# One kernel of retention attention, a gated MLP and capped expert routing: VectorE and ScalarE in written order in its first part

## The chip, the cores and the metric

The kernel runs on one core of a Trainium2 chip. The metric is device time in microseconds (us), from the kernel's start to its end. Times of one kernel are the median of several runs; the profile shows one execution of its own.

## The reference

Three stages on float32 data, each on the output of the last:

```
scores = q @ k^T / 8                        # 8 batches x 8 heads, 576 x 64
ret    = scores * gamma[h]^(i-j), i >= j    # decay, causal
x      = (ret @ v)  -> 4608 tokens x 512
a, b   = x @ w1, x @ w2                     # w1, w2: 512 x 1024
x      = ((a * b) @ w3) @ w_out             # w3: 1024 x 1024, w_out: 1024 x 512
logits = x @ w_gate                         # 8 experts
# tokens assigned greedily by descending logit, 576 tokens to an expert
out[tokens of e] = relu(x @ w1[e]) @ w2[e]  # expert widths 512 -> 1024 -> 512
```

w1, w2, w3 and w_out come as 64-bit words that hold double-precision values; the kernel makes pairs of 32-bit numbers of them, a rounded high part and a remainder.

## The kernel before

**Tiling.** The 4608 tokens are 36 attention tiles of 128 tokens; three tiles make a block of 384 (`TB`, 12 blocks). Attention is computed in chunks of 64 tokens with a running state, so tile t+1 needs the state of tile t. The MLP's first half, `ab(i)`, is one block's projections: for each of eight slices f of 128 columns one group of 12 matmuls for w1, copied out by ScalarE (L556), and one for w2, multiplied by that copy on VectorE (L558). Each matmul group goes over four row chunks and three products of high and low parts (L549).

**One attention tile** is a set of helpers: `att_scale` (two VectorE scalings, L261), `att_T` (transposes on TensorE, two copies on ScalarE, L276), `att_P` and `att_QK` (matmuls), `att_mask` (two VectorE products, L288), `att_state` (L310, L312), `att_AV` (L321, L329), `att_out` (ScalarE copy L337, VectorE sums L343 and L350, ScalarE rounding L344 and L349, GpSimd remainder L345). The output goes to the token block's x, in high and low parts. In `attention()` the step of tile t issues AV of t, then P, QK and mask of t+1, then the output of t, then the state of t+1 and the scaling and transposes of t+2.

**One weight unit** is 128 x 512 numbers. `conv(u)` makes it: magnitude on ScalarE (L196), clamp (L197), shift (L198), merge of sign (L200) and of low bits (L202) on VectorE, rounding copy on ScalarE (L215), remainder on VectorE (L216). Units are w1 and w2 in turn, slices 0 to 7 (16 units), then eight of w_out and sixteen of w3. A 1 MB load (`load_pair`) brings two slices of w1 or w2; four such loads have buffers at a time. `LEAD` says how many units ahead of its first use `ab(0)` converts.

**Order.** The Python program issues work from generators that `merge` and `turns` interleave by stated costs. That is the order of the program; the scheduler of the framework then orders each engine's instructions by its own model, with the program's order as priority, so that an engine may get a later instruction ahead of an earlier one. Each engine executes its queue in that order. The loads are issued from SP's queue (`ORDER`, then the calls in the generators). `begin()` is the first part: attention tiles 0 to 2 beside conversions, then block 0's projection beside tiles 3 to 5, then the rest of block 0 beside half of block 1; then `w34_all`, which converts w_out and w3, multiplies them, and is interleaved with blocks 1 to 3.

Of the kernel before, what the change touches and what calls it, by code (L numbers as in the profile page):

```python
# [15 lines left out]
TB, NB = 384, 12  # L16
PT = 96
EARLY, LATE0 = 4, 8
LEAD = (3, 4, 4, 4, 4, 4, 4, 4)
LATE = 1.25  # L20
TRIPS = 8
ROUNDS = ((0, 6), (-4, 6), (-4, 6), (-4, 6), (-5, 6))
ORDER = "q0 c0 k0 v0 c1 q1 k1 w0 v1 w1 q2 k2 v2 w2 w3 c2"
Q0 = 10
RAT = (0.75, 0.45, 0.35, 0.36)

# [58 lines left out]
def build(ctx, tc, io):  # L85
# [75 lines left out]
    raws = {}  # L161
# [19 lines left out]

    w3f = {}

    def conv(u):
        raw = raws.pop(u)
        lo, hi = raw[:, :, :, 0], raw[:, :, :, 1]
        if u[0] == "w3":
            b = 2048 + 512 * nxt("cv3", 2)
            ta = raw_t[:, b:b + 512]
        else:  # L190
            b = 512 * nxt("cv", 6)
            ta = tmp_t[:, b:b + 512]
        out = ta
        ta = ta.rearrange("p (k f) -> p k f", k=4)
        tb = hi.bitcast(F32)
        A.activation(ta, hi.bitcast(F32), AF.Abs)  # L196
        V.tensor_scalar(ta, ta, HIGH, LOW, op0=OP.min, op1=OP.max)  # L197
        V.tensor_scalar(ta.bitcast(I32), ta.bitcast(I32), 3, 0x3FFFFFF8,  # L198
                        op0=OP.logical_shift_left, op1=OP.bitwise_and)
        V.scalar_tensor_tensor(tb.bitcast(I32), hi, -1073741824, ta.bitcast(I32),  # L200
                               op0=OP.bitwise_and, op1=OP.bitwise_or)
        V.scalar_tensor_tensor(ta.bitcast(I32), lo, 29, tb.bitcast(I32),  # L202
                               op0=OP.logical_shift_right, op1=OP.bitwise_or)
        n, i, j = u
        if n == "w3":
            w3f[u] = out
            return
        hs, ls = SLOT(n)
        if n == "wo":
            hd, ld = hs[:, i, :], ls[:, i, :]  # L210
            fl = out
        else:
            hd, ld = (x[:, :, 128 * i:128 * i + 128] for x in (hs, ls))
            fl = ta
        A.activation(hd, fl, AF.Copy)  # L215
        V.tensor_tensor(ld, fl, hd.bitcast(F32), op=OP.subtract)  # L216


    qkv = [[A0[:, 1024 * j + 512 * i:1024 * j + 512 * i + 512] for j in range(3)] for i in range(2)]
# [8 lines left out]

    qkT = [A1[:, 1024 * i:1024 * i + 1024].rearrange("p (j c t) -> p j c t", j=2, c=4) for i in range(2)]
    AM = [A1[:, 2048 + 256 * i:2304 + 256 * i] for i in range(2)]  # L230
    ft = A1[:, 2560:3072].rearrange("p (s n) -> p s n", s=2)
    fk = [ft.rearrange("p s (u a i) -> p u s a i", u=2, a=2)[:, i] for i in range(2)]
    Sb = [A2[:, 768 + 256 * i:1024 + 256 * i] for i in range(3)]
    NT = N // 128

    loaded = set()

    def att_load(t, which=(0, 1, 2), eng=SP):
        for i in which:
            if t >= NT or (t, i) in loaded:  # L240
                continue
            loaded.add((t, i))
            x, src = buf(t)[i], (q, k, v)[i]
            p = 0
            while p < 128:
                b, s = divmod(128 * t + p, S)
                n = min(128 - p, S - s)
                if i == 2:
                    eng.dma_start(x[p:p + n].rearrange("p (h d) -> p h d", h=H),
                                 src[b, :, s:s + n, :].rearrange("h s d -> s h d"))  # L250
                else:
                    for r in range(2):
                        eng.dma_start(x[p:p + n].rearrange("p (c r d) -> p r c d", c=4, r=2)[:, r],
                                     src[b, 4 * r:4 * r + 4, s:s + n, :].rearrange("h s d -> s h d"))
                p += n

# [28 lines left out]

    def att_mask(t):
        for s in range(2):
            V.tensor_tensor(AM[s].rearrange("p (c i) -> p c i", c=4),  # L288
                            PYb[s][:, 0:256].rearrange("p (c i) -> p c i", c=4),
                            C("mask")[:, None, :].to_broadcast([128, 4, 64]), op=OP.mult)  # L290

# [22 lines left out]
    def att_AV(t):  # L314
        us = [u for u in range(2) if (2 * t + u) % 9]
        x = qkT[t % 2]
        for u in us:
            for a in range(2):
                for s, b in QUADS:
                    c = 2 * a + b  # L320
                    PE.matmul(PYb[s][halves(b), 256 + 128 * u + 64 * a:320 + 128 * u + 64 * a],  # L321
                              Sb[(2 * t + u) % 3][halves(s), 64 * c:64 * c + 64], x[halves(s), 0, c, halves(u)],
                              start=True, stop=True, skip_group_check=True)
        for s in range(2):
            for a in range(2):
                for u, b in QUADS:
                    c = 2 * a + b
                    k = 2 * s + a
                    PE.matmul(PX[u][halves(b), 64 * k:64 * k + 64],  # L329
                              buf(t)[2][halves(u), 256 * s + 64 * c:256 * s + 64 * c + 64],  # L330
                              AM[s][halves(u), 64 * c:64 * c + 64], start=True, stop=True, skip_group_check=True)

    def att_out(t):
        j, o = divmod(t, 3)
# [14 lines left out]
                A.activation(xh, po, AF.Copy)  # L349
                V.tensor_tensor(xl, po, xh.bitcast(F32), op=OP.subtract)  # L350

    def attention():
        def T(t):
            if t < NT:
                att_scale(t)
                att_T(t)
                if t != 2:
                    att_load(t + (3 if t < 2 else 2), (0,))
        T(0)
        T(1)  # L360
        att_P(0)
        att_QK(0)
        att_mask(0)
        att_state(0)
        yield 2500
        for t in range(NT):
# [10 lines left out]
            att_load(t + 3, (1,))  # L377
            if t != 2:
                att_load(t + (3 if t < 2 else 2), (2,))
            yield 1400  # L380


# [55 lines left out]
        V.tensor_reduce(WG[:, m, 0:8], p[:, :128].rearrange("p (c e) -> p e c", c=4)[:, :8], axis=AX.X, op=OP.add)  # L438
        yield 300

    units = [(n, i, 0) for i in range(8) for n in ("w1", "w2")] + [("wo", i, 0) for i in range(8)]
    units += [("w3", m, h) for m in range(8) for h in range(2)]
    nload = [0]
    nconv = [0]
# [1 line left out]
    def load_more(upto):  # L446

        upto = min(upto, len(units))
        n = 2 * ((upto - 1) // 4) + 2 if upto <= 16 else upto - 8
        while nload[0] < n:  # L450
            if nload[0] < 8:
                load_pair(nload[0])
            else:
                conv_load(units[nload[0] + 8])
            nload[0] += 1

    def conv_next():
        i = nconv[0]
        if i >= len(units):
            return False  # L460
        conv(units[i])
        nconv[0] += 1
        if i == 3:
# [5 lines left out]
        return True  # L469

    def conv_some(n):
        for _ in range(n):
            conv_next()
            yield 2500

    def w34_all():

        while nconv[0] < 25:
            conv_next()
            yield 2600  # L480
        hl = [w34_T(0, 0)]
        gate = None
        for m in range(8):
            for u in (2 * m + 1, 2 * m + 2):
                if u < 16:
                    conv_next()
                    hl.append(w34_T(*divmod(u, 2)))
                    yield 2600
            p = mm_bank()
# [44 lines left out]
    def ab(i):  # L534
# [3 lines left out]
        for f in range(8):  # L538
            fs = slice(128 * f, 128 * f + 128)
            for is_b in range(2):  # L540
                wh, wl = SLOT(("w1", "w2")[is_b])
                if i == 0:
                    need = units.index((("w1", "w2")[is_b], f, 0)) + LEAD[f]
                    while nconv[0] < min(need, 16):
                        conv_next()
# [5 lines left out]
                if not is_b:  # L551
                    if pend is not None:
                        split_g(i, pend)
                        pend = None
                    a = at_[nxt("a", 2)]
# [11 lines left out]
                yield 1960  # L567
        if pend is not None:
            split_g(i, pend)

# [479 lines left out]
            scat.append(st)  # L1050


    att = attention()
    PER = 3
    W34RATE = 1.0

# [24 lines left out]
        if side:  # L1081
            yield from side

    def turns(n, *gens):

        gens = list(gens)
        while gens:
            for g in gens[:]:
                for _ in range(n):
                    c = next(g, None)  # L1090
                    if c is None:
                        gens.remove(g)
                        break
                    yield c

    def begin():
        merge(take(6), conv_some(LEAD[0]), RAT[0])
        a0, a1 = ab(0), ab(1)
        s = take(2 * PER)
        merge(take_from(a0, 8), s, RAT[1])  # L1100
        drain(s)
        merge(turns(2, a0, take_from(a1, 8)), take(1), RAT[2])
        w = w34_all()
        merge(mix(a1, take(2 * PER - 1), 0.8), w, W34RATE)
        for i in range(2, EARLY):
            merge(mix(ab(i), take(2 * PER), RAT[3]), w, W34RATE)
        drain(w)
# [93 lines left out]
```

## Time and profile before

| what | value |
|---|---|
| median of 3 runs | 1313.09 us (1308.81 to 1315.04) |
| profiled execution | 1313.27 us, of which span 1311.2 us |
| busy in the span | TensorE 1257.6 us (96%), VectorE 530.5 (40%), ScalarE 461.0 (35%), GpSimd 253.8 (19%) |
| mean granted TensorE clock | 0.977 |
| TensorE in the first slice of 40 (32.8 us each) | busy 5 tenths, clock 7 tenths |
| in the second and third | 7 and 8 tenths, clock 7 and 9 tenths |
| VectorE in slices 1 to 4 | 6, 7, 9 and 6 tenths |

Busy time is the time in which an instruction of the engine runs. The span goes from the first to the last instruction; a slice is a fortieth of it. The granted clock is a share of TensorE's full speed, 1.00 at 2.4 GHz and 0.50 at 1.2.

### The profile page before, as it was taken

What the parts mean: (1) busy time and instruction counts of PE and PEld (TensorE: products, weight loads), DVE (VectorE), ACT (ScalarE), POOL (GpSimd) and SP (SyncE); (2) the same over time, 40 slices, a digit from 0 to 9 for tenths busy, and PEclk for the clock granted to TensorE, in tenths of its full rate; (3) what the DMA queues carried; (4) which work ended last, traced back from release to release, by engine and by line L of the source; (5) the groups of instructions that cost most, each with busy time, mean ns of one, the idle gap of its engine ahead of it and who ended that gap; (6) DMA issues with size and microseconds to landing.
All of it is one profiled execution on the core that took longest, in us unless ns stands there. A gap on an engine that the chain in (4) does not pass through costs nothing. (4 is left out here: it accounts for less than half of the span.)

```text
span 1311.2 us, 27175 instructions
## 1 busy us (share of the span) xinstructions
PE 1257.6 (96%) x11406; PEld 1114.9 (85%) x11406; DVE 530.5 (40%) x1298; ACT 461.0 (35%) x989; POOL 253.8 (19%) x238
## 2 busy tenths in 40 slices
PE   5789999999999999999999999879999999999996
PEld 4678988889898989889899777669989989899885
DVE  6796454433231312212212555453534425435220
ACT  4443333333322232212221544243434434435321
POOL 0101211112211120202011743331121211211011
PEclk7798999999999999999999999989999999999999
DMA  8766544422312131424012312163433525435110
GB/s 237 224 162 183 146 130 130 121 59 74 82 34 73 25 82 25 136 94 119 10 48 97 113 45 93 43 193 113 153 99 119 163 71 153 133 101 153 49 37 28
DMA packets 156382, 136.00 MB, mean 104 GB/s; under 512 B 119264, under 2 KB 119520, under 8 KB 155232
## 3 DMA queue, kind: packets, MB, share of 16 engines
q1 hardware_dynamic: 150368, 115.35, 30.1%
q0 software_dynamic: 5888, 18.88, 4.4%
q8 instruction: 91, 1.49, 0.5%
q14 instruction: 35, 0.29, 0.1%
HBM read 107.19 MB, written 27.00 MB: 102 GB/s over the span
## 5 line engine op out<-in xcount | busy, mean ns | idle before, releaser
L549 PE MATMUL p<-x,ws 128*128 128x384 f32 x2304 | 426.4, 341 | 1.1 <-POOL x L345 0.9
L549 PEld LDWEIGHTS p<-x,ws 128*128 128x128 f32 x2304 | 400.1, 189 | 9.4 <-issue 3.3
L1035 PE MATMUL p<-ws,g 128*128 128x512 f32 x864 | 218.1, 394 | 1.9 <-DVE rs L1045 1.4
L1035 PEld LDWEIGHTS p<-ws,g 128*128 128x128 f32 x864 | 156.6, 188 | 31.5 <-DVE rs L1045 1.8
L896 PE MATMUL p<-ws,x 128*128 128x512 f32 x576 | 141.8, 401 | 0.0
L896 PEld LDWEIGHTS p<-ws,x 128*128 128x128 f32 x576 | 105.7, 190 | 20.7 <-issue 0.4
L558 DVE TENSOR_TENSOR g<-p,ms 128x384 f32<-128x384 f32 x88 | 49.0, 557 | 181.7 <-PE p L549 173.6
L933 DVE TENSOR_TENSOR ws<-x,ws 128x512 fp32r<-128x512 f32 x120 | 80.9, 690 | 96.9 <-ACT ws L932 96.7
L261 POOL TENSOR_TENSOR a<-a,cst 128x512 f32<-128x512 f32 x52 | 54.8, 1053 | 302.4 <-DMA a<-q 239.7
L932 ACT ACTIVATE ws<-x 128x512 fp32r<-128x512 f32 x128 | 78.5, 630 | 72.3 <-DMA x<-ew 57.2
L556 ACT ACTIVATE ms<-p 128x384 f32<-128x384 f32 x96 | 46.9, 489 | 152.9 <-PE p L549 151.0
L345 POOL TENSOR_TENSOR x<-a,x 128x256 fp32r<-128x256 f32 x64 | 48.9, 775 | 262.5 <-ACT x L344 262.5
L1046 POOL DMA_INDIRECT out<-rs,idx x40 | 40.4, 1010 | 266.0 <-ACT g L1022 145.9
L601 PE MATMUL p<-ws,g 128*128 128x512 f32 x288 | 71.9, 398 | 0.0
L601 PEld LDWEIGHTS p<-ws,g 128*128 128x128 f32 x288 | 52.5, 188 | 13.3 <-issue 2.5
L1013 PE MATMUL p<-a,ws 128*128 128x320 f32 (+1 forms) x384 | 58.3, 301 | 0.5 <-ACT a L996 0.5
L1022 ACT ACTIVATE g<-py 128x256 fp32r<-128x256 f32 x96 | 31.5, 328 | 76.0 <-PE py L1013 67.4
L1013 PE MATMUL py<-a,ws 128*128 128x320 f32 (+1 forms) x384 | 57.4, 298 | 0.0
L1013 PE MATMUL py<-x,ws 128*128 128x320 f32 (+1 forms) x384 | 56.4, 296 | 0.3 <-DVE g L1023 0.3
L1013 PEld LDWEIGHTS p<-a,ws 128*128 128x128 f32 x384 | 55.0, 193 | 1.9 <-ACT a L996 0.7
L1013 PEld LDWEIGHTS py<-a,ws 128*128 128x128 f32 x384 | 54.9, 191 | 1.9
L1013 PE MATMUL p<-x,ws 128*128 128x320 f32 (+1 forms) x384 | 56.6, 297 | 0.0
(189 smaller groups left out, 1483.9 us busy)
## 6 DMA issues: line engine op xcount, KB each, us to landing
x<-ew SPq DMA_DIRECT2D x128, 256.0 KB, 3.1
y_scratch<-ms SPq DMA_DIRECT2D x36, 256.0 KB, 2.0
a<-k SPq DMA_DIRECT2D x64, 128.0 KB, 3.8
ws<-w SPq DMA_DIRECT2D x8, 1024.0 KB, 9.3
a<-q SPq DMA_DIRECT2D x62, 128.0 KB, 2.8
a<-v SPq DMA_DIRECT2D x31, 256.0 KB, 4.0
g_scratch<-g SPq DMA_DIRECT2D x8, 768.0 KB, 4.0
g<-g_scratch SPq DMA_DIRECT2D x4, 1536.0 KB, 6.8
```

Of the source, the lines that this page charges most:

```text
L261: (V if t < Q0 else G).tensor_tensor(xx, xx, tb_[:, :, None].to_broadcast([128, H, DH]), op=OP.mult)
L345: G.tensor_tensor(xl.rearrange("p (s a) i -> p s a i", s=2), f, xh.bitcast(F32).rearrange("p (s a) i -> p s a i", s=2), op=OP.subtract)
L549: PE.matmul(p[:, :TB], w[:, kk, fs], x[:, kk, :], start=(kk == 0 and j == 0), stop=(kk == 3 and j == 2))
L556: A.activation(a, p[:, :TB], AF.Copy)
L558: V.tensor_tensor(g[:, f, :], p[:, :TB], a, op=OP.mult)
L601: PE.matmul(p, x[:, f, ts], w[:, f, :], start=(f == 0 and j == 0), stop=(f == 7 and j == 2))
L896: PE.matmul(p, x[:, f, :], w[:, f, :], start=(f == 0 and j == 0), stop=(f == 7 and j == 2))
L932: A.activation(h, st, AF.Copy)
L933: low.tensor_tensor(lo[:, 512 * u:512 * u + 512], st, h.bitcast(F32), op=OP.subtract)
L1013: PE.matmul(p[:, :n], w[:, kk, fs], x[kk][:, ts], start=(kk == 0 and j == 0), stop=(kk == 3 and j == 2))
L1035: PE.matmul(p, x, w[:, f, :], start=(f == 0 and j == 0), stop=(f == 7 and j == len(ops) - 1))
L1046: st = G.indirect_dma_start(out=out, out_offset=bass.IndirectOffsetOnAxis(ap=idx[:n, 5 * e + o:5 * e + o + 1], axis=0), in_=ob[:n], in_off ...
```

## The change

Within `begin()`, from the first tile to the end of block 0, VectorE and ScalarE issue their instructions in the order of the program (`manual_schedule`); the other engines stay with the scheduler, and so does the place of later instructions among those of this part. Tiles 0 to 2 and 3 to 5 get a written order of their own, `att_three`, in which no tile outside the three takes part. `conv` is split into steps with yields between, and issues the next unit's magnitude (`conv_abs`) at its own start where that unit's load has been issued. The first units are w1 slices 0 and 1, then w2 slices 0 and 1, and four units stand among the first three tiles. The third and fourth weight loads leave the opening list and are queued behind the loads of tile 3's k and v. `LEAD` is 2 throughout; odd tiles below 6 mask into a second buffer (`AM2`); the attention generator starts at tile 6.

```
-LEAD = (3, 4, 4, 4, 4, 4, 4, 4)
+LEAD = (2, 2, 2, 2, 2, 2, 2, 2)
-ORDER = "q0 c0 k0 v0 c1 q1 k1 w0 v1 w1 q2 k2 v2 w2 w3 c2"
+ORDER = "q0 c0 k0 v0 c1 q1 k1 w0 v1 w1 q2 k2 v2 c2"
...
+        begun[u] = lo, hi, ta, tb, out
+
+    def conv(u, after=None):
+        if u not in begun:
+            conv_abs(u)
+        if after in raws and u[0] != "w3" and after[0] != "w3":
+            conv_abs(after)
+        lo, hi, ta, tb, out = begun.pop(u)
         V.tensor_scalar(ta, ta, HIGH, LOW, op0=OP.min, op1=OP.max)
+        yield 350
         V.tensor_scalar(ta.bitcast(I32), ta.bitcast(I32), 3, 0x3FFFFFF8,
                         op0=OP.logical_shift_left, op1=OP.bitwise_and)
+        yield 350
         V.scalar_tensor_tensor(tb.bitcast(I32), hi, -1073741824, ta.bitcast(I32),
                                op0=OP.bitwise_and, op1=OP.bitwise_or)
+        yield 600
...
         A.activation(hd, fl, AF.Copy)
+        yield 600
         V.tensor_tensor(ld, fl, hd.bitcast(F32), op=OP.subtract)
+        yield 600
...
+    def att_three(t):
+
+        att_scale(t)
+        yield 1200
+        att_T(t)
+        next_q(t)
+        att_scale(t + 1)
+        yield 1200
+        att_P(t)
+        att_QK(t)
+        att_T(t + 1)
+        next_q(t + 1)
+        yield 500
+        att_state(t)
+        att_mask(t)
+        yield 1300
+        att_P(t + 1)
+        att_QK(t + 1)
+        att_AV(t)
+        yield 300
+        att_mask(t + 1)
+        att_state(t + 1)
+        yield 1300
+        att_out(t)
+        next_kv(t)
+        yield 700
+        att_scale(t + 2)
+        yield 1200
+        att_T(t + 2)
+        next_q(t + 2)
+        yield 300
+        att_P(t + 2)
+        att_QK(t + 2)
+        att_AV(t + 1)
+        yield 300
+        att_mask(t + 2)
+        att_state(t + 2)
+        yield 1300
+        att_out(t + 1)
+        next_kv(t + 1)
+        yield 700
+        att_AV(t + 2)
+        yield 300
+        att_out(t + 2)
+        next_kv(t + 2)
+        yield 700
...
-    units = [(n, i, 0) for i in range(8) for n in ("w1", "w2")] + [("wo", i, 0) for i in range(8)]
+    units = [("w1", 0, 0), ("w1", 1, 0), ("w2", 0, 0), ("w2", 1, 0)]
+    units += [(n, i, 0) for i in range(2, 8) for n in ("w1", "w2")] + [("wo", i, 0) for i in range(8)]
...
-        merge(take(6), conv_some(LEAD[0]), RAT[0])
         a0, a1 = ab(0), ab(1)
-        s = take(2 * PER)
-        merge(take_from(a0, 8), s, RAT[1])
-        drain(s)
-        merge(turns(2, a0, take_from(a1, 8)), take(1), RAT[2])
+        with tc.manual_schedule(engines={V.engine, A.engine}):
+            c, s = conv_some(4), att_three(0)
+            drain(take_from(s, 5))
+            drain(take_from(c, 5))
+            drain(take_from(s, 2))
+            for n in range(2):
+                with tc.issue_after(loads[3, 1 + n].ins):
+                    load_more(8 if n else 7)
+            drain(take_from(c, 5))
+            drain(take_from(s, 2))
+            drain(take_from(c, 2))
+            drain(take_from(s, 1))
+            drain(take_from(c, 3))
+            drain(take_from(s, 2))
+            drain(take_from(c, 2))
+            drain(take_from(s, 1))
+            drain(c)
+            drain(s)
+            s = att_three(3)
+            merge(take_from(a0, 8 + FINE), s, RAT[1])
+            drain(s)
+            drain(mix(a0, take_from(a1, 8), 0.44))
         w = w34_all()
-        merge(mix(a1, take(2 * PER - 1), 0.8), w, W34RATE)
+        merge(mix(a1, take(2 * PER), 0.8), w, W34RATE)
```

## Rows read from the trace of the kernel before

**Rows 1.** Busy time by stretch: us, busy us (instructions) of each engine, granted clock, DMA share, GB/s.
```profile
core 0: us, PE busy (x) PEld busy (x) DVE busy (x) ACT busy (x) POOL busy (x), PEclk, DMA share, GB/s
0.00:47.25 47.25, 25.36 (x540) 20.97 (x540) 35.74 (x77) 19.71 (x37) 3.99 (x10) 0.69 0.78 201
47.25:85.82 38.57, 33.72 (x493) 30.38 (x494) 31.62 (x66) 19.83 (x39) 6.05 (x6) 0.94 0.74 225
85.82:117.12 31.30, 31.30 (x180) 31.00 (x180) 29.56 (x59) 13.17 (x24) 0.00 (x0) 1.00 0.56 178
117.12:160.00 42.88, 40.51 (x674) 36.78 (x674) 17.39 (x39) 14.43 (x29) 10.57 (x12) 0.92 0.58 162
```

**Rows 2.** Order of time on TensorE: start, us, engine, line, instruction, [idle before, releaser].
```profile
30.12 2.10 PE L329 MATMUL p<-a,g 64*64 64x64 f32 x32
...
47.25 6.91 PE L549 MATMUL p<-x,ws 128*128 128x384 f32 x24
...
85.82 31.37 PE L549 MATMUL p<-x,ws 128*128 128x384 f32 x179 [0.88 <-POOL x L345]
...
136.93 0.69 PE L321 MATMUL py<-a,a 64*64 64x64 f32 x32
...
138.95 1.31 PE L549 MATMUL p<-x,ws 128*128 128x384 f32 x6
```

**Rows 3.** Order of time on VectorE, 36 to 55 us.
```profile
36.13 0.41 DVE L198 TENSOR_SCALAR g<-g 128x512 int32<-128x512 int32 x1
36.47 0.68 DVE L202 SCALAR_TENSOR_TENSOR g<-ws 128x512 int32<-128x512 int32 x1
37.07 0.68 DVE L200 SCALAR_TENSOR_TENSOR ws<-ws,g 128x512 int32<-128x512 int32 x1
...
38.88 0.68 DVE L261 TENSOR_TENSOR a<-a,cst 128x512 f32<-128x512 f32 x1
...
43.43 0.74 DVE L288 TENSOR_TENSOR a<-py,cst 128x256 f32<-128x256 f32 x2
44.10 0.68 DVE L216 TENSOR_TENSOR ws<-g,ws 128x512 fp32r<-128x512 f32 x1
...
45.30 0.74 DVE L343 TENSOR_TENSOR a<-p,a 128x256 f32<-128x256 f32 x2
45.97 0.87 DVE L312 TENSOR_TENSOR a<-p,a 128x256 f32<-128x256 f32 x2
...
54.27 0.56 DVE L558 TENSOR_TENSOR g<-p,ms 128x384 f32<-128x384 f32 x1 [5.24 <-ACT g L196]
```

**Rows 4.** Order of time on ScalarE.
```profile
44.29 0.60 ACT L337 ACTIVATE a<-py 128x512 f32<-128x512 f32 x1 [0.25 <-DVE a L288]
```

**Rows 5.** Order of time on VectorE, the first weight unit.
```profile
15.23 0.43 DVE L197 TENSOR_SCALAR g<-g 128x512 f32<-128x512 f32 x1 [3.50 <-ACT g L196]
...
17.51 0.68 DVE L202 SCALAR_TENSOR_TENSOR g<-ws 128x512 int32<-128x512 int32 x1
...
18.89 0.69 DVE L216 TENSOR_TENSOR ws<-g,ws 128x512 fp32r<-128x512 f32 x1
```

**Rows 6.** Waits of VectorE, 60 to 145 us: us in total, times, longest.
```profile
DVE a L343 <- ACT a L337: 2.2, 3, 0.7
```

**Rows 7.** SP's queue in order of time, and the weight loads issued from 18.6.
```profile
16.54 2.03 SPq L249 DMA_DIRECT2D g<-v  x1
18.61 2.38 SPq L170 DMA_DIRECT2D ws<-w  x2
...
22.69 7.33 SPq L253 DMA_DIRECT2D a<-q  x6
...
62.70 0.93 SPq L253 DMA_DIRECT2D a<-q  x2
...
DMA to landing us min/median/max: 7.2/8.2/9.2
```

**Rows 8.** Busy time by stretch, two stretches of 10 us.
```profile
70.00:80.00 10.00, 7.27 (x170) 5.98 (x170) 10.00 (x21) 4.67 (x10) 1.26 (x1) 1.00 0.47 132
...
120.00:130.00 10.00, 7.63 (x77) 6.74 (x79) 2.11 (x6) 2.93 (x6) 2.96 (x4) 0.69 0.74 209
```

More of the change, by code (lines that the diff above doesn't have):

```diff
@@ L182, in build, with conv_abs @@
     w3f = {}
-    def conv(u):
+    begun = {}
+    def conv_abs(u):
         raw = raws.pop(u)
@@ L230, in build, with masked @@
     AM = [A1[:, 2048 + 256 * i:2304 + 256 * i] for i in range(2)]
+    AM2 = [RS[:, 512 + 256 * i:768 + 256 * i] for i in range(2)]
+    def masked(t):
+        return AM2 if t < 6 and t % 2 else AM
     ft = A1[:, 2560:3072].rearrange("p (s n) -> p s n", s=2)
@@ L236, in build @@
     loaded = set()
+    loads = {}
     def att_load(t, which=(0, 1, 2), eng=SP):
@@ L248, in att_load @@
                 if i == 2:
-                    eng.dma_start(x[p:p + n].rearrange("p (h d) -> p h d", h=H),
+                    loads[t, i] = eng.dma_start(x[p:p + n].rearrange("p (h d) -> p h d", h=H),
                                  src[b, :, s:s + n, :].rearrange("h s d -> s h d"))
@@ L252, in att_load @@
                     for r in range(2):
-                        eng.dma_start(x[p:p + n].rearrange("p (c r d) -> p r c d", c=4, r=2)[:, r],
+                        loads[t, i] = eng.dma_start(x[p:p + n].rearrange("p (c r d) -> p r c d", c=4, r=2)[:, r],
                                      src[b, 4 * r:4 * r + 4, s:s + n, :].rearrange("h s d -> s h d"))
@@ L330, in att_AV @@
                               buf(t)[2][halves(u), 256 * s + 64 * c:256 * s + 64 * c + 64],
-                              AM[s][halves(u), 64 * c:64 * c + 64], start=True, stop=True, skip_group_check=True)
+                              masked(t)[s][halves(u), 64 * c:64 * c + 64], start=True, stop=True, skip_group_check=True)
     def att_out(t):
@@ L350, in att_out, with next_q, next_kv, attention @@
                 V.tensor_tensor(xl, po, xh.bitcast(F32), op=OP.subtract)
-    def attention():
+    def next_q(t):
+        if t != 2:
+            att_load(t + (3 if t < 2 else 2), (0,))
+    def next_kv(t):
+        att_load(t + 3, (1,))
+        if t != 2:
+            att_load(t + (3 if t < 2 else 2), (2,))
+    def att_three(t):
[43 more added lines that the diff above has]
+        yield 700
+    def attention(first):
         def T(t):
@@ L356, in T @@
                 att_T(t)
[L357 to L364, printed above, removed]
+                next_q(t)
+        T(first)
+        T(first + 1)
+        att_P(first)
+        att_QK(first)
+        att_mask(first)
+        att_state(first)
         yield 2500
-        for t in range(NT):
+        for t in range(first, NT):
             att_AV(t)
@@ L376, in attention @@
             T(t + 2)
-            att_load(t + 3, (1,))
-            if t != 2:
-                att_load(t + (3 if t < 2 else 2), (2,))
+            next_kv(t)
             yield 1400
@@ L449, in load_more @@
         n = 2 * ((upto - 1) // 4) + 2 if upto <= 16 else upto - 8
+        n = 3 if upto == 7 else n
         while nload[0] < n:
@@ L458, in conv_next @@
         i = nconv[0]
-        if i >= len(units):
-            return False
-        conv(units[i])
         nconv[0] += 1
+        yield from conv(units[i], units[i + 1] if i < 23 else None)
         if i == 3:
@@ L468, in conv_next @@
             load_more(i + 4)
-        return True
     def conv_some(n):
         for _ in range(n):
-            conv_next()
-            yield 2500
+            yield from conv_next()
     def w34_all():
         while nconv[0] < 25:
-            conv_next()
+            drain(conv_next())
             yield 2600
@@ L485, in w34_all @@
                 if u < 16:
-                    conv_next()
+                    drain(conv_next())
                     hl.append(w34_T(*divmod(u, 2)))
@@ L544, in ab @@
                     while nconv[0] < min(need, 16):
-                        conv_next()
+                        yield from conv_next()
                 p = mm_bank()
@@ L554, in ab @@
                         pend = None
-                    a = at_[nxt("a", 2)]
+                    a = at_[nxt("a", 2) if i > 1 else i]
                     A.activation(a, p[:, :TB], AF.Copy)
@@ L566, in ab @@
                         again(2 * (i - LATE0) + 1)
-                yield 1960
+                yield 300 if i == 0 and f < 4 else 1960
         if pend is not None:
@@ L1050, in expert @@
             scat.append(st)
-    att = attention()
+    att = attention(6)
     PER = 3
@@ L1082, in mix @@
             yield from side
[L1084 to L1094, printed above, removed]
+    FINE = 25
     def begin():
-        merge(take(6), conv_some(LEAD[0]), RAT[0])
         a0, a1 = ab(0), ab(1)
-        s = take(2 * PER)
-        merge(take_from(a0, 8), s, RAT[1])
-        drain(s)
-        merge(turns(2, a0, take_from(a1, 8)), take(1), RAT[2])
+        with tc.manual_schedule(engines={V.engine, A.engine}):
[20 more added lines that the diff above has]
+            drain(mix(a0, take_from(a1, 8), 0.44))
         w = w34_all()
-        merge(mix(a1, take(2 * PER - 1), 0.8), w, W34RATE)
+        merge(mix(a1, take(2 * PER), 0.8), w, W34RATE)
         for i in range(2, EARLY):
```

2 lines of the change are left out of this document (1 added, 1 removed).

## The prediction

> **What bounds the kernel now.** I read the stages first, then TensorE's order of time in the first 145 us, and then, for each gap, the engine that ended it. TensorE is the limit of nearly the whole span, so only the stretches where it stands idle or runs at its lower clock can give anything back. The stages say where these are: in the first 47.25 us it is busy 25.36 us at a mean granted clock of 0.69, in the next 38.57 us it is busy 33.72 at 0.94, from 85.82 to 117.12 it has no gap, and in the 42.88 us after that 2.4 us are missing [rows 1]. Everything behind is solid, so the run's time should move by as much as TensorE's progress at about 115 us moves.
>
> The gap that costs most ends at 47.25, where the first projection matmul (L549) starts [rows 2]. It needs the first token block, tiles 0 to 2. Tile 2's last attention matmuls are over at 32.2 (30.12 + 2.10), but its output sums run at 45.30 [rows 2, 3]. Between them stands ScalarE's copy L337 at 44.29, released by VectorE's mask L288 at 43.43 [rows 3, 4]. That mask is tile 3's: in `attention()` the program issues tile t+1's QK and mask ahead of `att_out(t)`, and both read the same PSUM tile. Tile 3's mask waits for its transposes, and these for the scaling L261 that VectorE does at 38.88 in the middle of weight conversions [rows 3]. By then VectorE has converted eight units, of which the first projection group pair needs two. So tile 2 is finished 13 us after it could be, behind tile 3's chain and conversions that nobody waits for yet.
>
> **The change, part by part.** Prices on VectorE are the distances between starts. Of one unit: clamp 0.34, shift 0.34 (36.13 to 36.47), the two merges 0.60 each (36.47 to 37.07), the subtraction, of the same duration, 0.60 [rows 3], 2.48 in all. Where nothing stands between the second merge and the subtraction, VectorE waits for ScalarE's rounding copy: merge 17.51, subtraction 18.89, so 1.38 instead of 0.60, and the unit takes 3.26 [rows 5]. Of a tile: scaling 2 x 0.60, mask pair 0.67 (43.43 to 44.10), sums pair 0.67 (45.30 to 45.97) [rows 3], state pair, of the same form, 0.67: 3.2. Between mask and sums VectorE waits 0.75 for L337 [rows 6].
>
> *First three tiles.* The new order has no tile 3 among them, and four units in place of eight. Up to 15.23, where the first clamp gets its magnitude from the weights' load [rows 5], I take everything as before. Then in program order: unit 0, 3.26 (18.5); mask and state of tile 1, 1.34, wait and output of tile 0, 1.1 (20.9); unit 1, 3.26 (24.2); scaling of tile 2, 1.2 (25.4); unit 2's clamp and shift 0.7 (26.1) while TensorE transposes; its rest, with the rounding copy queued behind tile 2's two transposition copies, 2.9 (29.0); mask and state of tile 2, 1.34 (30.3); wait and output of tile 1, 1.5 (31.8); unit 3, 3.26 (35.1); sums of tile 2, 0.67 (35.8), and the first half of ScalarE's last copy: the projection starts at about 36 instead of 47.25, **11 us earlier**.
>
> One added wait stands in this chain: unit 3's step first issues unit 4's magnitude on ScalarE, and unit 4's weights are loaded only now. Behind that instruction are queued unit 3's rounding copy and tile 2's output copies, so the projection itself. The load used to be issued at 18.61 and moves behind the loads of q3, q4 and k3. Those were issued from 22.69 on, six in 7.33 us because the queue was full of the two weight loads; two take 0.93 where SP is free. With the weights gone I put them at 20.0 to 24.4 after v2 (16.54 + 2.03), c2 and the gate's weights, the weight load at 24.5, and its landing 7.2 to 9.2 later, at 31.7 to 33.7 [rows 7]. Unit 4's magnitude is wanted at 32.3. So the wait costs 0 to 1.4 us; I take 0 and keep 3 us (full queue as before) as the other end.
>
> *First half of the first projection.* The first 24 matmuls take 6.91 at half clock, as they did [rows 2], so from 36.2 to 43.1. VectorE's product of that pair stands in program order ahead of unit 4, so VectorE idles from about 37 to 43: the same stall as before, where the product came at 54.27 after 5.24 idle [rows 3]. From 43.1 to group pair 3 VectorE has units 4 to 8, 5 x 2.48 = 12.4; the waits for the rounding copy, 4 x 0.78 = 3.1 (the fifth is covered by tile 4's scaling); of tiles 3 to 5 what the ratio 0.45 lets in (the scalings of 4 and 5, masks and states of 3 and 4, output of 3): 5.75; four products of 0.47, 1.9; about 0.9 of waiting for the second product. Sum 24.0: 67.1. TensorE has 6 groups and two and a half tiles there and waits for units, some 4 us in all.
>
> *The rest of tile 5*, which is issued in one piece: transposes and copies 2.3, QK and mask 1.6, wait and sums of tile 4 1.4, its AV matmuls 1.1, copy, sums and rounding of tile 5 2.0, that is 8.4, nearly all a chain across engines: 75.5. By then TensorE has nine groups done (the ninth needs unit 8 alone and fits under the chain). Before, it had ten done at 85.82, where the solid stretch starts with 179 matmuls in 31.37, 2.10 a group of twelve [rows 2].
>
> *Second half.* Each unit now stands beside one group of block 0 and one of block 1. A pair of units and two products cost VectorE 2 x 3.26 + 2 x 0.47 = 7.5 against four groups, 8.4, on TensorE, so TensorE is again the limit and I expect no gap. 24 groups are due in all: 75.5 + 15 x 2.10 = 107.0 after, 85.82 + 14 x 2.10 = 115.2 before: **8.2 us gained**; 3 of the 11 went into the ordered queue.
>
> *What is late next.* Before, VectorE was 29.56 of 31.30 us busy in the solid stretch [rows 1], because the eight units of w_out and the first of w3 were pulled into it. After, 75.5 to 107.0 holds 7 units (17.4) and 8 products (3.8): 10 us are free, four of those nine units. Five, 12.4 us, come later, where VectorE had 17.39 busy of 42.88 [rows 1]: room enough, but they now stand before the w3 product, and tiles 6 to 8 share the queue. Between nothing and the 18 us of the third rival below I take 2, near the nearer end because of that room.
>
> *Clock.* In the chain of tile 5 TensorE does small transposes with gaps. A similar place before, 70 to 80 us, with 7.27 of 10 us busy, stayed at 1.00; another, 120 to 130, with 7.63, fell to 0.69 [rows 8]. The Trainium skill ("TensorE: Matmul & The Clock Gate", section on HAM oscillation) says that the lower clock is what the array falls back to when waits break up its work, and that each new burst then starts slow. The traces show it doing both; by the rule one more slow start would be paid. Priced by rows, 24 matmuls at 6.91 against 4.20, it is 2.7 us [rows 2]; I take 0 and keep 2.7 in the range.
>
> Sum: 8.2 - 2 = 6.2 us against the profiled execution of 1313.27 (span 1311.2), which lies 0.2 above the median of 1313.09: 1307.0.
>
> **The rivals.** *The whole lead stays* (0.20). If the scheduler fills VectorE's waits with w_out units and the projection's first half runs at TensorE's pace, the 11 us are kept: 1302, and up to 1299 if the 2.4 idle us behind 117 go too. For it: those waits are exactly gaps that later units can fill. Against: the product ahead of unit 4 still stalls VectorE, and loads of w_out are asked for only when unit 7 is done.
>
> *VectorE is the limit in both* (0.17). Its busy time up to 117 is 35.74 + 31.62 + 29.56 = 96.9 us of some 102 from 15.23 on [rows 1]; the same work in a stricter order, with up to 16 rounding waits of 0.78 = 12.5 us, ends no earlier: 1310 to 1316, about 1313. Against: nine units, 22 us of it, were not needed before 117.
>
> *The backlog bites* (0.13), on the slower side. If none of the nine later units slips into the ordered stretch, VectorE faces at 107 nine units of 3.26, 29.3, three tiles, 9.6, and four products, 1.9: 40.8 us. TensorE has for that time eight groups, 16.8, and three tiles of 2.0 (AV, P and QK from 136.93 to 138.95, transposes left out [rows 2]), 6.0: 22.8. It would stand up to 18 us: 10 slower than before, 1323. It decides from a surplus of 8.2 us on. For it: the order is fixed on just the two engines that convert. Against: the second block follows its tiles, not w3's product, and the order binds only what is issued inside that part.
>
> **How the numbers follow.** The forecast, a gain of 3 to 10 us (1303 to 1310), has 0.50. The runs before spread over 6 us, so 0.5%, 6.6 us, is about what can be told from no change; the bound lies at 1306.5, inside the forecast's own range, and I give 0.22 of its half below it and 0.28 above. Faster: 0.22 + 0.20 = 0.42. Slower by over 0.5% needs more than 1319.7: 0.10 of the third rival. Same: 0.28 + 0.17 + 0.03 = 0.48. The range 1300 to 1316 holds the forecast, most of the first rival, and the second, with the 3 us of the load and the 2.7 of the clock; it leaves the third out.
>
> **What will show it.** The first L549 matmul at about 36 (right between 34 and 39; past 41 the load's wait decides, and ScalarE's L196 shows a wait on the weights' DMA ahead of it). VectorE idle some 6 us ahead of its first product. In the first projection's half, waits of VectorE on the rounding copy of 0.8 each. TensorE solid from about 75 on, with block 0 and half of block 1 done near 107. Wrong would be: TensorE waiting on VectorE for several us behind 107, or the projection's start unmoved.

## The result, and the profile after

The changed kernel takes 1327.63 us (1327.30 to 1327.87), the kernel before 1313.12 us beside it: ratio 1.0116, 95% interval 1.0095 to 1.0138. It is 14.5 us slower, outside my range, and on the side to which I gave 0.10. The span grew by 13.9 us (1311.2 to 1325.1).

Where the 13.9 us arise, by TensorE's idle time (stretch less busy) in the four stages of [rows 1]: before 21.89, 4.85, 0.00 and 2.37, in all 29.1; after 23.86, 7.64, 0.48 and 6.83, in all 38.8. So 5.2 us are lost ahead of 117 and 4.5 in the 43 us behind it. Another 0.8 of idle time comes later (53.6 us over the span before, 64.1 after), and 3.4 are longer busy time (1257.6 to 1261.0). Busy time by stage after (columns as in [rows 1]), and the 10 us of [rows 8] whose clock fell:

```profile
0.00:47.25 47.25, 23.39 (x443) 20.84 (x444) 24.95 (x50) 14.28 (x27) 5.17 (x11) 0.75 0.88 234
47.25:85.82 38.57, 30.93 (x498) 26.42 (x498) 29.73 (x58) 14.69 (x30) 3.86 (x5) 0.91 0.67 192
85.82:117.12 31.30, 30.82 (x240) 28.48 (x239) 25.91 (x52) 14.71 (x28) 0.00 (x0) 1.00 0.22 60
117.12:160.00 42.88, 36.05 (x554) 31.59 (x553) 39.79 (x78) 20.39 (x40) 11.14 (x11) 0.92 0.68 200
70.00:80.00 10.00, 7.80 (x181) 6.86 (x182) 5.33 (x10) 2.87 (x7) 1.71 (x3) 0.66 0.88 270
```

The third column of busy times says most. VectorE did 96.92 us of work up to 117 before, and 80.59 after: 16.3 us less, although it was the scarce engine there. Behind 117 it has 39.79 in place of 17.39. The work did not get less; it came later. Of the eight units of w_out, all eight had their second merge by 111.9 us before; by 117 after, two had (L215 at 102.07 and 107.20).

TensorE in order of time after, against [rows 2] (the projection is L621 now, output sums and rounding L364 and L365, the rounding copy L228):

```profile
39.07 0.69 PE L621 MATMUL p<-x,ws 128*128 128x384 f32 x1 [4.45 <-ACT x L365]
40.94 8.04 PE L621 MATMUL p<-x,ws 128*128 128x384 f32 x35 [1.18 <-POOL x L366]
...
65.78 2.76 PE L621 MATMUL p<-x,ws 128*128 128x384 f32 x12 [1.91 <-ACT ws L228]
72.19 1.29 PE L295 MATMUL p<-cst,a 64*128 64x64 f32 x16 [3.65 <-DVE a L282]
...
84.06 2.19 PE L621 MATMUL p<-x,ws 128*128 128x384 f32 x11
...
134.94 2.38 PE L621 MATMUL p<-x,ws 128*128 128x384 f32 x12 [2.21 <-ACT ms L628]
...
146.58 0.70 PE L465 MATMUL p<-cst,g 128*128 128x128 f32 x4 [2.00 <-ACT a L297]
148.34 1.09 PE L465 MATMUL p<-cst,g 128*128 128x128 f32 x4 [1.06 <-DVE g L215]
```

The projection does start 8.2 us earlier (39.07 against 47.25), but its second matmul waits for GpSimd, and the lead goes: the tenth group of twelve ends at 86.2 here (with the row at 84.06) and at 84.8 before. Later milestones, before and after: first matmul of the w34 product 149.0 and 158.8, first y matmul 335.3 and 347.4, last projection 710.2 and 722.2. From there on the shift stays between 12 and 14.

VectorE after, against [rows 3] (product L630; clamp, shift, merges L207, L209, L212, L215; remainder L230; scaling L282; state L333; sums L364):

```profile
31.83 0.95 DVE L333 TENSOR_TENSOR a<-p,a 128x256 f32<-128x256 f32 x2 [1.58 <-PE p L350]
...
33.81 0.85 DVE L209 TENSOR_SCALAR g<-g 128x512 int32<-128x512 int32 x1
34.69 1.09 DVE L212 SCALAR_TENSOR_TENSOR ws<-ws,g 128x512 int32<-128x512 int32 x1
...
38.48 1.82 DVE L282 TENSOR_TENSOR a<-a,cst 128x512 f32<-128x512 f32 x2
...
47.01 0.56 DVE L630 TENSOR_TENSOR g<-p,ms 128x384 f32<-128x384 f32 x1 [6.70 <-PE p L621]
...
52.45 0.42 DVE L207 TENSOR_SCALAR g<-g 128x512 f32<-128x512 f32 x1
52.90 0.43 DVE L209 TENSOR_SCALAR g<-g 128x512 int32<-128x512 int32 x1
53.36 0.69 DVE L212 SCALAR_TENSOR_TENSOR ws<-ws,g 128x512 int32<-128x512 int32 x1
54.09 0.69 DVE L215 SCALAR_TENSOR_TENSOR g<-ws 128x512 int32<-128x512 int32 x1
55.48 0.69 DVE L230 TENSOR_TENSOR ws<-g,ws 128x512 fp32r<-128x512 f32 x1 [0.70 <-ACT ws L228]
...
71.46 1.28 DVE L282 TENSOR_TENSOR a<-a,cst 128x512 f32<-128x512 f32 x2
...
80.45 0.69 DVE L282 TENSOR_TENSOR a<-a,cst 128x512 f32<-128x512 f32 x1 [2.06 <-DMA a<-q]
...
82.26 0.42 DVE L364 TENSOR_TENSOR a<-p,a 128x256 f32<-128x256 f32 x1 [0.45 <-PE p L350]
```

A unit in strict order (52.45 to 56.09) takes 3.64: starts 0.45, 0.46 and 0.73 apart, then 1.39 to the remainder and 0.61. At 80.45 the scaling of a later tile stands in the queue and waits 2.06 for its load, in the midst of tile 5's chain. VectorE's three largest waits after, 13 to 117 us (us in total, times, longest):

```profile
DVE ws L230 <- ACT ws L228: 8.2, 11, 1.2
DVE g L630 <- PE p L621: 7.5, 3, 6.7
DVE rs L309 <- PE py L342: 2.5, 1, 2.5
```

### The profile page after: what moved, and what is told of

It reads as the page before. It is cut to its first block, busy times and chain, and to the rows that moved or that the text cites. A ratio compares the mean times of both kernels' runs of the same rounds, so it can differ in the third digit from the quotient of the medians.

```text
span 1325.1 us, 27187 instructions
## 1 busy us (share of the span) xinstructions
PE 1261.0 (95%) x11406; PEld 1114.1 (84%) x11406; DVE 538.8 (41%) x1298; ACT 458.8 (35%) x989; POOL 255.9 (19%) x238
## 5 line engine op out<-in xcount | busy, mean ns | idle before, releaser
L621 PE MATMUL p<-x,ws 128*128 128x384 f32 x2304 | 428.6, 340 | 11.7 <-ACT x L365 4.5
L621 PEld LDWEIGHTS p<-x,ws 128*128 128x128 f32 x2304 | 398.5, 189 | 22.2 <-ACT x L365 4.6
L630 DVE TENSOR_TENSOR g<-p,ms 128x384 f32<-128x384 f32 x88 | 48.9, 556 | 187.8 <-PE p L621 183.8
L282 POOL TENSOR_TENSOR a<-a,cst 128x512 f32<-128x512 f32 x52 | 56.3, 1083 | 343.4 <-DMA a<-q 218.1
L1005 DVE TENSOR_TENSOR ws<-x,ws 128x512 fp32r<-128x512 f32 x120 | 80.6, 690 | 97.7 <-ACT ws L1004 97.4
L1118 POOL DMA_INDIRECT out<-rs,idx x40 | 39.8, 995 | 266.2 <-ACT g L1094 145.9
```

The source lines that it names most:

```text
L282: (V if t < Q0 else G).tensor_tensor(xx, xx, tb_[:, :, None].to_broadcast([128, H, DH]), op=OP.mult)
L621: PE.matmul(p[:, :TB], w[:, kk, fs], x[:, kk, :], start=(kk == 0 and j == 0), stop=(kk == 3 and j == 2))
L1005: low.tensor_tensor(lo[:, 512 * u:512 * u + 512], st, h.bitcast(F32), op=OP.subtract)
L1118: st = G.indirect_dma_start(out=out, out_offset=bass.IndirectOffsetOnAxis(ap=idx[:n, 5 * e + o:5 * e + o + 1], axis=0), in_=ob[:n], in_off ...
```

## The experiments

Two theories at first. *The order*: VectorE and ScalarE, bound to the program's order, stand behind waits that the scheduler filled with other work. *The arrangement*: the new places of units, loads and magnitudes cost the time, under any order. Within the first, *early* (TensorE starves ahead of 117) stood against *late* (VectorE's work piles up behind it).

**The order taken away** (e1_free).

```
-        with tc.manual_schedule(engines={V.engine, A.engine}):
+        if True:
```

> The changed kernel with nothing but the fixed order taken away: VectorE and ScalarE are the scheduler's again, the new tile order, the four first units, the later weight loads and the early magnitude stay. Theory A (the fixed order costs VectorE: a unit whose steps follow each other takes about 3.6 us instead of 2.5, sixteen units 18 us, paid between 117 and 160): the lead of the first tiles stays without the price, 1300 to 1310 us, and VectorE is not busy for more than 25 of the 43 us behind 117. Theory B (what costs is the new arrangement: too few units early, VectorE standing ahead of the first product): little better than the changed kernel, 1320 to 1330 us, with VectorE idle for some 6 us ahead of its first L630.

1311.73 us, 1.0007 (0.9996 to 1.0018), just past Theory A's range and far from Theory B's. The order is the whole loss, and the arrangement alone is worth nothing. Its stages, and its largest waits of VectorE from 13 to 117:

```profile
0.00:47.25 47.25, 28.73 (x508) 25.51 (x509) 28.98 (x64) 18.21 (x34) 5.23 (x11) 0.89 0.89 236
47.25:85.82 38.57, 31.85 (x463) 27.10 (x462) 37.39 (x76) 20.61 (x39) 7.45 (x5) 0.97 0.65 189
85.82:117.12 31.30, 30.92 (x250) 29.60 (x249) 29.12 (x59) 14.98 (x27) 0.00 (x0) 0.98 0.56 181
117.12:160.00 42.88, 40.63 (x687) 36.87 (x686) 21.32 (x49) 15.39 (x32) 10.54 (x12) 0.96 0.62 162
```

```profile
DVE g L207 <- ACT g L198: 4.1, 1, 4.1
DVE g L630 <- PE p L621: 3.3, 2, 3.2
```

The projection starts at 37.6, as early as in the changed kernel, and VectorE is busy 37.39 of the 38.57 us behind 47.25. Even so nothing is gained. That reads as my second rival, VectorE the limit in both, once the order is left out; it is not shown, for the runs that were to show it by relieving VectorE (e8_free_q3, e9_free_gsub below) were slower themselves.

**How much of the part is ordered** (e2_first, e7_half): the order ends behind the first three tiles, and behind tile 5.

```
             drain(s)
-            s = att_three(3)
-            merge(take_from(a0, 8 + FINE), s, RAT[1])
-            drain(s)
-            drain(mix(a0, take_from(a1, 8), 0.44))
+        s = att_three(3)
+        merge(take_from(a0, 8 + FINE), s, RAT[1])
+        drain(s)
+        drain(mix(a0, take_from(a1, 8), 0.44))
```

```
-            drain(mix(a0, take_from(a1, 8), 0.44))
+        drain(mix(a0, take_from(a1, 8), 0.44))
```

> The fixed order ends behind tile 2, so it covers four units of the sixteen. Theory A: a quarter of the price, four units of 1.1 us, lies in a stretch where VectorE has waits anyway; 1302 to 1312 us. Theory B: as the changed kernel, 1322 to 1330 us, because the first stage, with its four units, is the same.

> The fixed order ends behind tile 5, so that the second half of block 0 with half of block 1 is free again. If the backlog arises in that second half (seven units in strict order, the units of w_out kept out): 1313 to 1319 us. If it is made before, in the stretch with tiles 3 to 5 (waits ahead of the first product, tile 5 in one piece): 1320 to 1327 us.

1316.62, 1.0046 (1.0029 to 1.0063), and 1324.34, 1.0087 (1.0064 to 1.0111). The first lies between its two ranges, the second in its upper one. With none and all of it: 0.07, 0.46, 0.87 and 1.16%. Each of the three parts costs 0.3 to 0.4%, none of them the whole.

**Which engine** (e13_dve_only, e14_act_only).

```
-engines={V.engine, A.engine}
+engines={V.engine}
```

and `{A.engine}` in the other.

> The changed kernel with VectorE alone in fixed order; ScalarE is the scheduler's again. If VectorE's queue carries the price (steps behind what they depend on, products that wait for TensorE at its head): 1323 to 1329 us, as with both. If ScalarE's queue does (a magnitude waiting for a load ahead of the tiles' copies, copies behind rounding copies): 1312 to 1318 us.

> The counterpart: ScalarE alone in fixed order. If VectorE's queue carries the price: 1310 to 1315 us, like the version without a fixed order. If ScalarE's does: 1322 to 1328 us. In between for both says that each queue alone holds part of it.

Both came out as forecast for VectorE's queue. VectorE alone: 1328.16, 1.0118 (1.0091 to 1.0144), all of the loss. ScalarE alone: 1314.98, 1.0027 (1.0014 to 1.0040), little, and nothing that adds to VectorE's.

**The same order on the arrangement of before** (e4_ordered), around the same part of `begin()`.

```
+        with tc.manual_schedule(engines={V.engine, A.engine}):
+            merge(take(6), conv_some(LEAD[0]), RAT[0])
...
+            merge(turns(2, a0, take_from(a1, 8)), take(1), RAT[2])
```

> The kernel before with one thing done to it: in the first part, up to the end of block 0, VectorE and ScalarE issue in the program's order. Its tile order, units, loads and magnitudes are those of before. Theory A (a fixed order costs by itself, through steps that follow what they depend on): clearly slower, 1325 to 1345 us, more than the changed kernel, whose order was written for it. Theory B (the order costs only together with the new arrangement): 1308 to 1318 us.

1344.46, 1.0244 (1.0221 to 1.0267), in Theory A's range. The new arrangement repairs half of what the order costs on the old one. There, TensorE's largest waits from 47 to 117 are for ScalarE's copy of a:

```profile
PE p L549 <- ACT ms L556: 16.8, 4, 7.4
```

**The waits at the head of VectorE's queue, one at a time.** A lead of four units, so that VectorE has units to convert ahead of the first product (e3_lead4); two units' steps in turn, so that no step follows the one it depends on (e5_pairs); both (e15_pairs_lead4).

```
-LEAD = (2, 2, 2, 2, 2, 2, 2, 2)
+LEAD = (4, 4, 4, 4, 4, 4, 4, 4)
...
-    FINE = 25
+    FINE = 35
```

```
+        gens = [conv(units[j], units[j + 2]) for j in (i, i + 1)]
+        for _ in range(5):
+            for g in gens:
+                yield next(g)
...
-    FINE = 25
+    FINE = 30
```

The third has both, with FINE 40. In the pairs the next units' magnitudes are issued behind the rounding copies.

> The changed kernel with four units of lead instead of two, so that two units stand ahead of the first product on VectorE and fill its wait of 6.7 us; the fixed order stays. Theory B: the 6.7 us come back nearly whole, 1319 to 1323 us. Theory A: VectorE gains at most the same 6.7 us of work but each unit still costs 3.6, so that the backlog behind 117 shrinks only by that: 1320 to 1326 us. A result at or above 1327 says that the wait ahead of the first product was not on the path.

> The changed kernel with the fixed order kept, but two units converted at a time with their steps in turn, so that no step on VectorE follows the one it depends on, and the next magnitudes issued behind the rounding copies. Theory A: 16 units cost about 2.6 instead of 3.6 us, some 16 us of VectorE, and the backlog behind 117 goes: 1308 to 1317 us. Theory B: the steps' distances shrink but TensorE waits as before for tile 5's chain and the first product: 1322 to 1328 us.

> Fixed order kept, two units at a time with their steps in turn, and four units of lead, so that a pair stands ahead of the first product. Both repairs of VectorE's queue together: if its waits add up (the lead alone gave back a tenth of a per cent at most, the pairs 5 us), 1314 to 1319 us. If each repair only hands the wait on to the next instruction at the head: 1319 to 1325 us, no better than the pairs alone.

The lead alone: 1324.62, 1.0121 (1.0087 to 1.0156), nothing back that shows within this interval. The pairs: 1321.43, 1.0079 (1.0062 to 1.0096), between the two ranges. Both: 1317.46, 1.0049 (1.0035 to 1.0063), as forecast, more than half of the loss back. The lead alone took away the wait of 6.7 ahead of the first product, but turned part of it into another; its largest waits of VectorE up to 160, and of TensorE for VectorE's products, which the changed kernel does not have, from 13 to 117:

```profile
DVE ws L230 <- ACT ws L228: 11.2, 11, 3.2
```

```profile
PE p L621 <- DVE g L630: 4.3, 3, 3.0
```

With both, VectorE goes from pair to pair and meets the first product (L647) without a wait; its waits for rounding copies up to 117 are 2.8 us in 3 (8.2 in 11 in the changed kernel), two of them in this stretch:

```profile
41.41 0.75 DVE L207 TENSOR_SCALAR g<-g 128x512 int32<-128x512 int32 x2
42.08 1.28 DVE L210 SCALAR_TENSOR_TENSOR ws<-ws,g 128x512 int32<-128x512 int32 x2
...
47.54 0.69 DVE L230 TENSOR_TENSOR ws<-g,ws 128x512 fp32r<-128x512 f32 x1 [1.76 <-ACT ws L226]
48.61 0.69 DVE L230 TENSOR_TENSOR ws<-g,ws 128x512 fp32r<-128x512 f32 x1 [0.38 <-ACT ws L226]
49.22 0.55 DVE L647 TENSOR_TENSOR g<-p,ms 128x384 f32<-128x384 f32 x1
```

and behind 117 VectorE has 27.04 us of work instead of 39.79, TensorE 40.63 instead of 36.05:

```profile
117.12:160.00 42.88, 40.63 (x676) 36.65 (x678) 27.04 (x58) 17.30 (x34) 11.52 (x12) 0.96 0.66 195
```

**Work taken from VectorE.** Scaling of tiles 6 to 9 on GpSimd (e6_q6: Q0 10 to 6); the remainders of w_out there (e10_wo_gsub); those of units 4 to 15 (e11_unit_gsub), so that the rounding copy is waited for by GpSimd.

```
-        V.tensor_tensor(ld, fl, hd.bitcast(F32), op=OP.subtract)
+        (G if n == "wo" else V).tensor_tensor(ld, fl, hd.bitcast(F32), op=OP.subtract)
```

with `u in units[4:16]` in e11_unit_gsub.

> The changed kernel with the scaling of tiles 6 to 9 on GpSimd instead of VectorE, eight instructions of 0.6 us, 4.8 us off VectorE around and behind 117; nothing of the order changes, and scalings of later tiles can no longer stand in VectorE's queue and wait for a load. Backlog theory (behind 117 VectorE is the limit): 3 to 6 us come back, 1321 to 1324.5 us. Rival (TensorE's waits there are a chain across engines and not VectorE's load): no change, 1326 to 1329 us.

> The changed kernel, fixed order and all, with the last step (the remainder) of the eight units of w_out on GpSimd instead of VectorE: 8 x 0.6 = 4.8 us off VectorE in just the stretch from 99 to 141 where it does them, with GpSimd idle there. Backlog theory (behind 99 VectorE is the limit): 3 to 5 us come back, 1322 to 1325 us. Rival (the lost time lies ahead of 90, in the waits of the ordered stretch, and what follows only carries it on): 1326 to 1328.5 us.

> The changed kernel with the remainder of units 4 to 15 of w1 and w2 on GpSimd. VectorE's queue then holds no step that waits for ScalarE's rounding copy, and 0.6 us less work a unit; the clamp, shift and merges still follow each other at 0.46, 0.46 and 0.72. If the wait for the rounding copy at the head of the ordered queue is the price: 12 x 1.3 = 15 us of VectorE less, most of the loss comes back, 1312 to 1319 us. If the price is the waits ahead of products and tile 5's chain: 1322 to 1327 us.

In this order: 1326.20 us, 1.0111 (1.0091 to 1.0131); 1325.97, 1.0107 (1.0077 to 1.0138); 1329.26, 1.0121 (1.0096 to 1.0145): no gain in any. The first two lie at the lower edge of "no change", the last above either expectation. They are weak tests of the backlog, for they hardly shortened it: behind 117 VectorE stays busy 39.90, 37.02 and 36.97 us. In the last the wait moved instead of going. From 40 to 130 VectorE waits 13.2 us for products (7.8 in the changed kernel), and TensorE waits for GpSimd's remainders:

```profile
PE p L621 <- POOL ws L230: 2.9, 5, 0.7
```

**The same relief without the order** (e8_free_q3: e1_free with Q0 = 3; e9_free_gsub and e12_before_gsub: the remainders of units 4 to 23 on GpSimd in e1_free and in the kernel before).

> No fixed order, and the scaling of tiles 3 to 9 on GpSimd: 14 instructions of 0.6 us, 8.4 us, off VectorE, which in the version without a fixed order is 37.39 of 38.57 us busy between 47 and 86, where that version loses its lead. If VectorE is the limit of that stretch, up to 5 us are gained on it: 1305 to 1310 us. If the chain of each tile is (a scaling takes 1.05 on GpSimd instead of 0.6, and stands in each tile's chain twice): 1311 to 1316 us.

> The new arrangement without a fixed order, with the remainders of units 4 to 23 on GpSimd: 12 us off VectorE, which in the version without a fixed order is 37.39 of 38.57 us busy from 47 to 86 and 29.12 of 31.30 behind. If VectorE's load is what takes back the lead of the first tiles there: 1303 to 1308 us. If it is the chain of the tiles, or the remainder arrives too late on GpSimd (1.05 instead of 0.6, in line with the tiles' own remainders): 1311 to 1317 us.

> The kernel before with the same remainders on GpSimd, as the counterpart of the last one. VectorE is busy nearly without a break from 15 to 48 and from 56 to 117 there. If its load is the limit of the first part whatever the arrangement: 1303 to 1308 us, like the other. If the lead of the new arrangement is what becomes usable: this one 1309 to 1313 us and the other at least 3 us less.

In this order: 1318.16 us, 1.0050 (1.0033 to 1.0067); 1324.31, 1.0087 (1.0064 to 1.0110); 1323.84, 1.0081 (1.0057 to 1.0105): all slower, and each outside both of its expectations. GpSimd is no cover for VectorE here, and no version beats both kernels.

**Early or late.** Sums over the stages of each profile, which is one execution: TensorE idle ahead of and behind 117.12 us (up to 160), VectorE busy ahead of it and behind.

| kernel | ratio | TensorE idle ahead | behind | VectorE busy ahead | behind |
|---|---|---|---|---|---|
| before | 1 | 26.7 | 2.4 | 96.9 | 17.4 |
| after | 1.0116 | 32.0 | 6.8 | 80.6 | 39.8 |
| e1_free | 1.0007 | 25.6 | 2.3 | 95.5 | 21.3 |
| e7_half | 1.0087 | 36.9 | 2.9 | 99.7 | 27.2 |
| e5_pairs | 1.0079 | 28.7 | 8.8 | 85.8 | 35.4 |
| e15_pairs_lead4 | 1.0049 | 30.2 | 2.3 | 91.3 | 27.0 |
| e3_lead4 | 1.0121 | 32.6 | 4.8 | 90.5 | 32.7 |
| e14_act_only | 1.0027 | 22.4 | 5.6 | 89.3 | 31.5 |
| e4_ordered | 1.0244 | 46.7 | 5.5 | 70.6 | 37.0 |

Both happen, and a loss of 0.8 to 0.9% comes with either alone: e7_half loses 10.1 us ahead and next to nothing behind, e5_pairs 1.9 ahead and 6.5 behind. The changed kernel has about half of each, 5.2 and 4.5. The late loss goes with the backlog in all the profiles, those left out of the table too: where VectorE is busy 31.5 us or more behind 117, TensorE is idle 4.8 or more there, and where VectorE has 27.2 or less, at most 2.9. That is a correlation; no run changed the backlog alone. The early loss is not always an idle VectorE: in e7_half VectorE is busy all through tile 5's chain with steps of later units that the scheduler put between, and the chain takes 12.6 us (77.07 to 89.70).

## Why the prediction was wrong

The step that failed is the sum of the second half with "What is late next": 8.2 us of lead at group 24 less 2 for the backlog. The runs show group 24 ending 7.0 later than before instead, the lead gone at the tenth group, and a loss of 4.5 us behind 117. Step by step:

- **First three tiles**, projection at 36: it started at 39.07, and in earnest at 40.94. Ahead of tile 2's state VectorE waited 1.58 for TensorE (31.83). Unit 3's steps beside GpSimd's remainder of tile 1 took 0.85 and 1.09 where they take 0.43 and 0.69 alone, and GpSimd's own remainder of tile 2, which I had left out, held the second matmul 1.18.
- **Unit 4's load**, 0 taken: right. Issued at 24.98 (24.5 predicted); the magnitude that needs it ran at 33.80 with no wait on a DMA:

```profile
24.98 1.15 SPq L170 DMA_DIRECT2D ws<-w  x2
```

```profile
33.80 0.66 ACT L198 ACTIVATE g<-ws 128x512 f32<-128x512 f32 x1
```

- **VectorE idle some 6 us ahead of the first product**: right, 6.70. But I had priced this only on TensorE's path. It is also VectorE work that is not done, and it comes back behind 117.
- **A unit at 3.26** and the rounding waits: the waits came (0.70 each, 11 of them), but a strict unit takes 3.64. My prices were distances between *independent* steps [rows 3]; each dependent step starts about 0.12 later. The 1.38 from the second merge to the subtraction [rows 5] was right by luck: in the trace before, two steps of a tile stand between the two; the changed kernel has 1.39 where nothing does. A state pair, taken as 0.67, is 0.87 in [rows 3] itself.
- **First half, 24.0**: from the first product to tile 5's scaling 47.01 to 71.46, 24.5. Right in size, the dearer units and the tiles' steps that hid some of their waits evening out, but from a start 3.9 later.
- **Tile 5 in one piece, 8.4**: 71.46 to about 82.6, 11.1, with the pulled-in scaling (2.06) and a slow clock. Nine groups were done at 83.3, not 75.5.
- **Clock at 0**: wrong. TensorE stood 3.65 us at 72.19 for the scaling, and 70 to 80 was granted 0.66, between its levels of 1.2 and 2.4 GHz, where the same 10 us had 1.00 before [rows 8]. The rule of the Trainium skill that I set aside ("TensorE: Matmul & The Clock Gate", section on HAM oscillation) agrees. What it cost I can't separate: TensorE's busy time is 3.4 us longer over the span (2.7 was my price for one slow start), at the same mean clock of 0.977.
- **Second half solid**: right from 84 on, 0.48 us idle up to 117. The 24 groups ended at 122.1, 7.0 later than before (115.1; I had 107.0): 1.5 were lost by the tenth, and 5.0 are tile work of block 2 pulled in between, which I had put at nothing there (eleven rows of L295, L304, L321 and L350 from 86.18 to 119.78, summed).
- **Late next, 2**: mis-sized; TensorE lost 4.5 behind 117. I counted the seven units of the second half at 2.48 (17.4 us), though a paragraph earlier a unit in strict order cost 3.26; at the 3.64 measured they take 25.5 of the 31.5 us. So two units of w_out came ahead of 117, not four of the nine ahead of 107. The third rival had the direction right, but not the size: TensorE stood far less than its 18 us there, and that its 1323 lies near 1327.6 is in part luck, for half of the loss arose ahead of 117. My argument for the near end was VectorE's "room" in [rows 1]; that room was there only because the scheduler had filled VectorE's waits earlier, which is just what the change forbids.

The first rival, the whole lead kept, fell even without the order: e1_free ended no earlier. That VectorE's order is the cause is shown, by e1_free, e13_dve_only and the steps between. That dependent steps, rounding waits and the idle time ahead of the product carry a good part of it is what e15_pairs_lead4 points to; it changed pairs, lead, FINE and the place of the magnitudes together, so their shares are not shown. How the 14.5 us split exactly between starving ahead and backlog behind stays open: the runs that were to take the backlog away alone (e6_q6, e10_wo_gsub) did not shorten it enough. The profile of e2_first does not help: its TensorE idle time up to 160 (27.1) is less than before, but the profiled execution took 1310.35 us, the shortest of a kernel whose median is 1316.62.

## What to carry to other kernels

When an order is fixed on an engine, price each wait at the head of its queue twice: what it delays on the critical path, and how much work of that engine it pushes behind the stage, which has to fit there. An engine that a scheduler keeps 94% busy (29.56 of 31.30 us) has little room to be idle 6 us, even where the bound engine is another. This is argued from the profiles. If an order is fixed, interleave independent units and give the engine work ahead of each wait, both together: the lead alone brought nothing that could be told, the pairs 0.37%, both 0.67% (differences of the ratios).

## What the runs showed of the hardware

VectorE's 128x512 steps start 0.34 and 0.60 us apart when independent, about 0.46 and 0.72 when each needs the one before. GpSimd and VectorE can slow each other when both work: beside the two rows below VectorE's shift took 0.85 for 0.43, its merge 1.09 for 0.69, and a scaling pair 1.82 for 1.28. GpSimd's own pair took 2.12 in the second row, against 1.43 at 134.29 of the kernel before. VectorE's steps that read a PSUM tile (p or py) kept their time: in the changed kernel, beside one pair of GpSimd's from 145.79 to 147.65, the state step L333 at 145.98 took 0.41, and the merge L215 at 147.10 took 1.10.

```profile
33.64 1.60 POOL L366 TENSOR_TENSOR x<-a,x 128x256 fp32r<-128x256 f32 x2 [11.96 <-ACT x L365]
38.76 2.12 POOL L366 TENSOR_TENSOR x<-a,x 128x256 fp32r<-128x256 f32 x2 [3.52 <-ACT x L365]
```

In e6_q6 one scaling on GpSimd stood beside a shift that took three times its 0.43:

```profile
65.72 1.04 POOL L282 TENSOR_TENSOR a<-a,cst 128x512 f32<-128x512 f32 x1 [8.53 <-DMA a<-k]
```

```profile
65.78 1.27 DVE L209 TENSOR_SCALAR g<-g 128x512 int32<-128x512 int32 x1
```

And GpSimd's remainder of a unit in e10_wo_gsub took 1690 ns against VectorE's 690:

```profile
L230 POOL TENSOR_TENSOR ws<-g,ws 128x512 fp32r<-128x512 f32 x8 | 13.3, 1690 | 39.1 <-DVE g L215 34.1 <-ACT ws L228 5.0
```

The Trainium skill ("GPSIMD Engine Reference", specifications) says that the two share their SBUF interfaces, with contention where VectorE works in a two-port mode or has two SBUF inputs. The merge and the scaling have two, and the rows agree and give the price; which case the shift is, with one input, no run here shows.
